# An RWKV layer and eight balanced experts on one core: where the split halves of gathered rows are kept, and where two groups of sums stand on the vector engine

## The chip, the cores and the metric

The kernel runs on one core of one Trainium2 chip. The metric is the device time of one execution in microseconds (us). Before the change it is 396.36 us, the median of three runs (396.04 to 397.14). The core's engines are named as the profile names them: PE (TensorE, matrix products), PEld (its weight loads), DVE (VectorE), ACT (ScalarE), POOL (GpSimd) and SP (SyncE, which here issues DMAs). Each engine works through its own instructions in the order in which they were compiled.

## The reference

Two stages follow one another. The first is an RWKV attention with a decaying state, for 4 sequences, 8 heads, 768 steps and a head width of 48:

```
for t in range(S):
    cur = einsum('bhd,bhe->bhde', u * k[t], v[t])
    y[t] = einsum('bhd,bhde->bhe', r[t], state + cur)
    state = w * state + einsum('bhd,bhe->bhde', k[t], v[t])
```

Its output is laid out as 3072 rows (tokens) of 384 numbers. The second stage assigns each row to one of 8 experts, 384 rows to each, by going through all gate values in falling order and giving a row to an expert as long as the row is free and the expert isn't full. Each expert then computes two matrix products on its rows:

```
logits = x @ w_gate
order = argsort(-logits.flatten())        # greedy: row free, expert not full
for e in range(E):
    h[mask_e] = maximum(x[mask_e] @ w1[e], 0)     # 384 -> 1024
    out[mask_e] = h @ w2[e]                       # 1024 -> 384
```

## The kernel before, in words

**Stages.** In the first part, up to about 150 us, the attention, the gate and a first pick of 256 rows of one expert (called the star expert) are written in a fixed order. Then the function `run` goes through the experts in the order in which the search finds them full: number 0 (the 256 early rows), 1 to 7 with three blocks of 128 rows each, and 8, the last 128 rows of the star expert. From there on a scheduler in the compiler orders the instructions of each engine: what is written first goes first if the scheduler's own clock says that its inputs are there, and what is written later fills the gaps. `tc.issue_after(ins)` ties what is written inside it behind the instruction `ins` on that instruction's engine.

**The search** (`likely_steps`, line 1025 on) finds the next full expert: three rounds of counting, each a product `counts` on PE (lines 949 and 960) between small DVE operations, then `acc` (line 1076), the rows taken, and the product `st_ps` (lines 1080 and 1081), which gives each row its place. `tokens` (line 1396 on) turns places into row numbers: DVE makes `row`, `oh` and `vals`, PE multiplies them (`some_ps`, line 1413), DVE adds (`some`, then `part`, line 1422), PE multiplies once more (`list_ps`, line 1431), and DVE writes `tok`. Then POOL gathers the rows (line 1521) and SP loads the expert's `w1` and `w2` (line 1514). The generator `later` is advanced a step at a time while the expert before it computes; `walk` is the search object. Expert 7 needs no search (`remainder`, line 1363), only the list.

**Two sets of tiles.** `self.turns` holds two pools with one buffer per name: rows `xg`, turned rows `xT`, `w1` and `w2`. Expert n uses pool n % 2.

**Turning the rows.** PE needs the rows with the 384 features on the partitions. Experts 1 and 5 are turned by PE. For 2, 3, 4, 6, 7 and 8 `turned_by_transfers` (line 1544) does it for each block: ACT splits the 4-byte numbers into 2-byte halves (`apart`, line 1551, a pool of two buffers), a DMA transpose issued by SP writes the halves back over the rows `xg` (line 1553), and ACT joins them into `xT` (line 1558). `turn_begins` starts this and `turn` ends it. The splits and joins are tied by `behind` to the last recorded copy `self.copied`. For experts with `seven` as second layer the splits begin after the product P6. For experts 6 and 7 they begin when `progress` passes 1.3, some way into the fifteen products.

**First layer.** Experts 1, 2, 4, 5 and 8 use `hidden` (line 1641): 8 banks of plain products. Experts 3, 6 and 7 (`FIRST_BY_SEVEN`) use `hidden_by_seven` (line 1593), a scheme with seven half-size products instead of eight, done twice (p = 0 and 1). It needs five sums of the turned rows, S1 to S5 (`row_sums`, line 1576, tiles `first_S`), and four sums of `w1`, T1 to T4 (`weight_sums`, line 1565, tiles `first_T`). The order of its products is

```
FIRST = {"P1": (("a0", "b0"),), "P2": (("a1", "b2"), ("d0", "c0")), "P5": (("d1", "c1"), ("S1", "T1")), ...
FIRST_ORDER = ("P1", 0), ("P2", 0), ("P5", 0), ("P6", 0), ("P1", 1), ("P7", 0), ("P3", 0), ("P4", 0), ...
```

so the second half of the third product (line 1625, `hb_ps<-first_S,first_T`) is the first to read S1 and T1. P1's `h_ps` and P2's `hc_ps` and the first half of P5 read `xT` and `w1` alone. ACT and DVE combine the products (`kept_P`, lines 1609, 1613 and 1617).

**Second layer.** Experts 1 to 5 use `seven` for two blocks and a plain product (`o_ps`, line 1783) for the third. Experts 6 and 7 use `fifteen`: fifteen products (line 1756) in four groups on sums of the hidden layer (`HID_SUMS`, eleven sums H) and of `w2` (`W2_SUMS`, ten sums W), then 20 output sums (line 1765) on DVE. All these sums are made at line 1697. For the experts with `seven`, `SEVEN_EARLY` is one sum of the hidden layer at its half. POOL scatters the results (line 1777).

**What stands where in the program before.** While expert n computes, `row_sums` for expert n+1 is written directly after `turn`, so ahead of what is left of the search and of the list of rows that follow it; `weight_sums` for n+1 is written as soon as `progress` passes 1.1.

Of the kernel before, what the change touches and what calls it, by code (L numbers as in the profile page):

```python
# [736 lines left out]
class Assignment:  # L737
# [24 lines left out]
    def __init__(self, ctx, tc, ML, CAP, C):  # L762
        self.tc, self.nc, self.ML, self.CAP, self.C = tc, tc.nc, ML, CAP, C
# [48 lines left out]
        self.ps = ctx.enter_context(tc.tile_pool(name="s_ps", bufs=1, space=PSUM))  # L812
        self.between = lambda: None
# [211 lines left out]
    def likely_steps(self, fmax, acc, place, on_fmax=None):  # L1025
# [50 lines left out]
        nc.vector.scalar_tensor_tensor(out=acc, in0=em, scalar=fmax, in1=past, op0=ALU.is_equal, op1=ALU.mult)  # L1076
# [319 lines left out]
    def tokens(self, place, NC=None):  # L1396
# [24 lines left out]
        with nc.allow_low_precision(reason="whole numbers up to 2048"):  # L1421
            nc.vector.tensor_reduce(out=part, in_=some.rearrange("p i h -> p h i"), axis=AX.X, op=ALU.add)
# [31 lines left out]
def rwkv5_eagle_then_base_layer_balanced(  # L1454
# [34 lines left out]
    class Experts:  # L1489
# [8 lines left out]
        def open_rest(self, ctx, **how):  # L1498
# [3 lines left out]
            self.apart = pool("f_apart", 1, **how)  # L1502
# [41 lines left out]
        def turned_by_transfers(self, ahead):  # L1544
            n, xg, tok = ahead[:3]
            xT = self.turns[n % 2].tile([128, KD, CAP], F32, name="xT")
            nb, halves = tok.shape[1], []
            for c in range(nb):
                apart = self.apart.tile([128, 2, DX], U16, name="apart", bufs=2)
                with self.behind():  # L1550
                    nc.scalar.copy(apart, xg[:, c, :].bitcast(U16).rearrange("p (f h) -> p h f", h=2))
# [4 lines left out]
            for c, turned in enumerate(halves):  # L1556
                with self.behind():
                    nc.scalar.copy(xT[:, :, ts(c, 128)].bitcast(U16).rearrange("p k (t h) -> p k t h", h=2),  # L1558
                                   turned.rearrange("p (h k) t -> p k t h", h=2))
# [33 lines left out]
        def hidden_by_seven(self, x, w, progress):  # L1593
# [18 lines left out]
            def block(p, i, f, src):  # L1612
                nc.scalar.activation(hid[:, ds(f * KF // 2 + p * Q, Q), ts(i, H)], src, AF.Relu)  # L1613
# [27 lines left out]
        def hidden(self, w1, xT, m, half, progress, lead=False):  # L1641
            hid = self.h.tile([128, KF, CAP], F32, name="hid")
            for js in [range(2) if lead else range(1), *([j] for j in range(2 if lead else 1, KF))]:
# [6 lines left out]
                for j in js:  # L1650
                    nc.scalar.activation(hid[:, j, 0:m], h_ps[j][:, 0:m], AF.Relu)  # L1651
# [143 lines left out]
        def run(self, ahead, later, rows, pulls={}, xT=None):  # L1795
            xT, lead = xT or self.turn(ahead), True
            row_sums = weight_sums = None
            while ahead:
# [12 lines left out]
                none = lambda: None  # L1811
                begins = [1.3]
                due = [1.55, 1.75] if some == 2 else [0.75 + 1.15 * i / (some - 1) for i in range(some)]

                def half(hid):
                    nonlocal right
# [4 lines left out]
                    last = self.sums_of(left, self.SEVEN_EARLY)  # L1821
                    if late:
                        with tc.issue_after(last.ins):
                            right = self.seven_w2(w2)
# [8 lines left out]
                def turn():  # L1833
                    nonlocal xT, row_sums
                    if ahead:
                        xT = next(pieces) if by_transfers else self.turn(ahead)
                        if after:
                            row_sums = self.row_sums(xT)

                def progress(t):  # L1840
                    nonlocal weight_sums
                    if after and t > 1.1 and not weight_sums:
                        weight_sums = self.weight_sums(ahead[3])
                    if many and begins and t > begins[0]:
                        begins.pop()
                        turn_begins()
# [14 lines left out]
                if many:  # L1861
                    self.sums_of(left, self.HID_SUMS)
# [198 lines left out]
```

## Time and profile before

| what | value |
|---|---|
| median of three runs | 396.36 us (396.04 to 397.14) |
| the profiled execution | 396.48 us, of which the span from first to last instruction is 394.7 us |
| mean granted TensorE clock | 0.992 |
| busy: DVE, ACT, POOL | 280.8 us (71%), 188.4 us (48%), 140.4 us (36%) |
| splits `apart` | 16, 834 ns each |
| transposes issued by SP | 16, median 2.8 us from issue to landing |
| joins `xT<-xg` | 16, 919 ns each |

A timeline row gives the start in us from the span's start, the duration in us, engine, line, operation, what is written from what, its size, how many were merged into the row, and in square brackets how long the engine stood idle before it and for what. Starts of neighbouring rows tell the pace; durations overlap, since the engines are pipelined. In a view of windows the columns are: the stretch, its length, then for each engine its busy time and its number of instructions, the granted TensorE clock (1.00 is full), the DMA share, and GB/s.

### The profile page before, as it was taken

To read this page: it belongs to the slowest core of one execution; us is meant where nothing else is said; L and a number is where in the kernel's file an instruction comes from. 1 tells how busy PE (TensorE), PEld (TensorE's weight loads), DVE (VectorE), ACT (ScalarE), POOL (GpSimd) and SP (SyncE) were. 2 spreads that over 40 slices of the span, in tenths; PEclk is the share of its full clock that TensorE was granted. 3 is DMA by queue.
4 is the path that set the end of the run, shared out by engine and by line. 5 is a ranking of instruction groups with operands and counts; after the bars stand their busy time and mean duration, and the time that the engine had idled before them with its cause. 6 is when DMAs were issued, how large, how long until landed. Compare 5 with 4: busy or idle time off the path is not lost.

```text
span 394.7 us, 9805 instructions
## 1 busy us (share of the span) xinstructions
PE 375.8 (95%) x3729; PEld 303.6 (77%) x3729; DVE 280.8 (71%) x959; ACT 188.4 (48%) x468; POOL 140.4 (36%) x173
## 2 busy tenths in 40 slices
PE   8899999999999999999999799999999998999993
PEld 7678888888877766686577798558657778989981
DVE  6755777586885787986867759889378964994530
ACT  4997989888873312235225343421212533544320
POOL 7878887676732022033022121203203230041020
PEclk9999999999999999999999899999999999999998
DMA  9999999787792174644644461309209573382110
GB/s 120 159 183 182 196 198 206 159 175 147 145 317 81 42 253 165 213 169 101 238 160 103 153 247 41 80 2 330 89 22 334 145 253 148 60 317 84 23 62 27
DMA packets 108136, 60.51 MB, mean 153 GB/s; under 512 B 90032, under 2 KB 102320, under 8 KB 108080
## 3 DMA queue, kind: packets, MB, share of 16 engines
q1 hardware_dynamic: 104736, 50.35, 51.7%
q0 software_dynamic: 3104, 9.44, 7.0%
q8 instruction: 31, 0.51, 0.5%
q14 instruction: 25, 0.20, 0.2%
q10 hardware_dynamic: 240, 0.00, 0.0%
HBM read 47.20 MB, written 9.44 MB: 143 GB/s over the span
## 4 chain that ended last, share of the span: by engine, by line
PE 56%; issue 16%; DVE 9%; DMA 7%; ACT 5%; POOL 5%; POOLq 0%; another core or an unknown queue 0%; DVEq 0%; ACTq 0%
PE h_ps L1648 12%; PE y_ps L546 5%; PE g_ps L506 4%; PE pa_ps L1722 4%; PE h_ps L1625 3%; DMA xg<-apart 3%; PE hb_ps L1625 3%; DMA xg<-x_rows,tok 3%; PE e_h_ps L1891 3%; PE o_ps L1783 3%; ACT AT L496 2%; PE kT_ps L459 2%; PE kv_ps L525 2%; PE pb_ps L1722 2%; PE x_ps L596 2%
## 5 line engine op out<-in xcount | busy, mean ns | idle before, releaser
L1648 PE MATMUL h_ps<-xT,w 128*128 128x384 f32 (+1 forms) x264 | 73.0, 427 | 0.2 <-ACT hid L1651 0.2
L496 ACT ACTIVATE AT<-ident,dd 128x128 f32<-128x128 f32 x192 | 59.6, 392 | 1.9 <-DVE dd L449 1.8
L1648 PEld LDWEIGHTS h_ps<-xT,w 128*128 128x128 f32 x264 | 42.1, 191 | 20.1 <-issue 2.3
L1521 POOL DMA_INDIRECT xg<-x_rows,tok x22 | 23.0, 1046 | 94.1 <-DVE own_c L1446 33.9
L1777 POOL DMA_INDIRECT out_dram<-o_all,to x16 | 19.0, 1186 | 89.6 <-DVE o_all L1765 44.8
L1651 ACT ACTIVATE hid<-h_ps 128x384 f32<-128x384 f32 (+1 forms) x40 | 17.9, 448 | 55.0 <-PE h_ps L1648 51.3
L513 DVE COPY_PREDICATED AT<-mask,g_ps 64x512 f32<-64x512 uint8 (+1 forms) x48 | 32.4, 725 | 11.9 <-PE g_ps L506 9.8
L1783 PE MATMUL o_ps<-w,hid 128*128 128x384 f32 x96 | 33.2, 489 | 0.0
L506 PE MATMUL g_ps<-rT,kT 48*64 48x128 f32 (+1 forms) x768 | 26.3, 255 | 1.8 <-DVE AT L513 1.0
L437 POOL TENSOR_TENSOR kss<-krs,wk 128x384 f32<-128x384 f32 x24 | 24.4, 1017 | 8.2 <-DVE krs L341 5.0
L546 PE MATMUL y_ps<-AT,vts 128*64 128x128 f32 x384 | 25.7, 276 | 0.0
L1783 PEld LDWEIGHTS o_ps<-w,hid 128*128 128x128 f32 x96 | 17.6, 190 | 9.9 <-issue 0.6
L444 POOL TENSOR_TENSOR rk<-rk,u_bc 128x384 f32<-128x384 f32 x24 | 24.1, 1005 | 1.9
L443 POOL TENSOR_TENSOR rk<-krs 128x384 f32<-128x384 f32 x24 | 24.6, 1023 | 0.3 <-DMA krs<-in_r_dram 0.3
L506 PEld LDWEIGHTS g_ps<-rT,kT 48*64 48x64 f32 x768 | 20.7, 132 | 5.1 <-PE unread_ps L419 0.9
L546 PEld LDWEIGHTS y_ps<-AT,vts 128*64 128x64 f32 x384 | 20.6, 137 | 1.0 <-issue 0.5
L1613 ACT ACTIVATE hid<-kept_P 128x384 f32<-128x384 f32 x18 | 9.4, 523 | 19.9 <-DVE kept_P L1617 17.9
L478 DVE TENSOR_TENSOR rT<-rT_ps,WR 112x512 f32<-112x512 f32 x23 | 15.7, 684 | 4.2 <-PE rT_ps L459 4.2
L449 DVE TENSOR_REDUCE dd<-rk 128x8 f32<-128x384 f32 x24 | 13.1, 546 | 6.5 <-POOL rk L444 6.5
L565 ACT COPY x<-y_ps 128x512 f32<-128x512 f32 x24 | 14.1, 586 | 7.3 <-PE y_ps L546 6.2
L1558 ACT COPY xT<-xg 128x768 uint16<-128x768 uint16 x16 | 14.4, 919 | 3.9 <-DMA xg<-apart 3.7
L459 PE MATMUL rT_ps<-ident,krs 128*112 128x128 f32 x96 | 15.4, 281 | 0.5 <-ACT krs L345 0.3
(342 smaller groups left out, 853.9 us busy)
## 6 DMA issues: line engine op xcount, KB each, us to landing
w<-in_moe_w_dram SPq DMA_DIRECT2D x18, 1536.0 KB, 7.0
krs<-in_k_dram SPq DMA_DIRECT2D x24, 192.0 KB, 3.8
krs<-in_r_dram SPq DMA_DIRECT2D x24, 192.0 KB, 5.1
vts<-in_v_dram SPq DMA_DIRECT2D x24, 192.0 KB, 5.1
x_rows<-xr SPq DMA_DIRECT2D x24, 192.0 KB, 2.0
xg<-x_rows,tok POOLq DMA_INDIRECT x22, 5.0
xg<-apart SPq DMA_TRANSPOSE x16, 2.8
out_dram<-o_all,to POOLq DMA_INDIRECT x16, 2.9
```

What stands on the lines that cost most here:

```text
L437: self.nc.gpsimd.tensor_mul(self.kss[:, n % self.NS].rearrange("p (g h) d -> p g h d", g=2)[:, :, :, 0:D], src, self.wk.rearrange("p (g h) ...
L443: nc.gpsimd.tensor_mul(rk, self.krs[:, n % self.NK, 1, 0:H, 0:D], self.krs[:, n % self.NK, 0, 0:H, 0:D])
L444: nc.gpsimd.tensor_mul(rk, rk, self.u_bc)
L459: self.nc.tensor.transpose(ps[0:PD + self.D, a, :], self.pair(t, a), self.ident)
L496: nc.scalar.mul(AT[:, z, a, :], self.ident, dd[:, h:h + 1])
L506: nc.tensor.matmul(g_ps[ts(i, PD), z, a, i * PD:], kT[rows, a, ts(i, PD)], rT[rows, a, i * PD:], start=True, stop=True)
L513: nc.vector.copy_predicated(out=AT[keys, :, :, steps], mask=mask, data=g_ps[keys, :, :, steps])
L546: nc.tensor.matmul(yv[q * PD:(q + 1) * PD, o // 2, o % 2, :], lhsT, rhs, start=(o // 2, q) not in seen, stop=stop, skip_group_check=True)
L1625: nc.tensor.matmul(ps[:, q, :], w[b][:, ts(p * Q + q, 128)], x[a], start=fresh, stop=(a, b) == pairs[-1], skip_group_check=True)
L1648: nc.tensor.matmul(h_ps[j][:, at], w1[:, f, ts(j, 128)], xT[:, f, at], start=(f == 0), stop=(f == KD - 1))
L1722: nc.tensor.matmul(ps, left[a][:, j, :], right[b][:, j, :], start=(j == 0 and name in ("P1", "P2", "P5")), stop=(j == KF // 2 - 1), skip_g ...
L1783: nc.tensor.matmul(o_ps, hid[:, j, ts(c, 128)], w2[:, j, :], start=(j == 0), stop=(j == KF - 1))
```

## The change

1. The pool `apart` is gone. The halves are written into the tile of rows of the other set, the pool (n + 1) % 2: three blocks have three places, where there were two buffers.
2. `row_sums` is no longer written after `turn` when the rows are turned by transfers (so for experts 3, 6 and 7). It is written at the start of the expert itself, after the rest of the search and the list for the expert behind it have been written, and tied behind `walk.taking`: the search's `acc`, or, from expert 7 on, where `rest` is set, the list's `part`.
3. `weight_sums` is tied behind `summed`, the last sum of the layer's rows: the sum of `SEVEN_EARLY`, or the last of `HID_SUMS`.
4. Where the second layer is `fifteen`, the splits are written ahead of its products, and the first layer's copies now count as `self.copied`.

```diff
+        self.taking = nc.vector.scalar_tensor_tensor(out=acc, in0=em, scalar=fmax, in1=past, op0=ALU.is_equal,
+                                                     op1=ALU.mult)
...
     def remainder(self):
+        self.rest = True
...
-            nc.vector.tensor_reduce(out=part, in_=some.rearrange("p i h -> p h i"), axis=AX.X, op=ALU.add)
+            listing = nc.vector.tensor_reduce(out=part, in_=some.rearrange("p i h -> p h i"), axis=AX.X, op=ALU.add)
+        if self.rest:
+            self.taking = listing
...
-            self.apart = pool("f_apart", 1, **how)
...
-            nb, halves = tok.shape[1], []
-            for c in range(nb):
-                apart = self.apart.tile([128, 2, DX], U16, name="apart", bufs=2)
+            halves = self.turns[(n + 1) % 2].tile([128, NC, DX], F32, name="xg")
+            for c in range(tok.shape[1]):
+                rows, apart = xg[:, c, :].bitcast(U16), halves[:, c, :].bitcast(U16)
                 with self.behind():
-                    nc.scalar.copy(apart, xg[:, c, :].bitcast(U16).rearrange("p (f h) -> p h f", h=2))
-                turned = xg[:, c, :].bitcast(U16).rearrange("p (g t) -> p g t", t=128)
-                nc.sync.dma_start_transpose(out=turned, in_=apart.rearrange("p h f -> p (h f)"))
-                halves.append(turned)
+                    nc.scalar.copy(apart.rearrange("p (h f) -> p h f", h=2), rows.rearrange("p (f h) -> p h f", h=2))
+                nc.sync.dma_start_transpose(out=rows.rearrange("p (g t) -> p g t", t=128), in_=apart)
...
-                nc.scalar.activation(hid[:, ds(f * KF // 2 + p * Q, Q), ts(i, H)], src, AF.Relu)
+                self.copied = nc.scalar.activation(hid[:, ds(f * KF // 2 + p * Q, Q), ts(i, H)], src, AF.Relu)
...
-                sums = dict(row_sums or {}, **weight_sums) if weight_sums else None
+                ahead = next((a for a in later if a), None)
+                if weight_sums and not row_sums:
+                    with tc.issue_after(walk.taking.ins):
+                        row_sums = self.row_sums(xT)
+                sums = dict(row_sums, **weight_sums) if weight_sums else None
                 row_sums = weight_sums = None
-                ahead = next((a for a in later if a), None)
...
-                    last = self.sums_of(left, self.SEVEN_EARLY)
+                    summed = self.sums_of(left, self.SEVEN_EARLY)
...
-                        if after:
+                        if after and not by_transfers:
                             row_sums = self.row_sums(xT)
...
                     if after and t > 1.1 and not weight_sums:
-                        weight_sums = self.weight_sums(ahead[3])
-                    if many and begins and t > begins[0]:
-                        begins.pop()
-                        turn_begins()
+                        with tc.issue_after(summed.ins):
+                            weight_sums = self.weight_sums(ahead[3])
...
                 if many:
-                    self.sums_of(left, self.HID_SUMS)
+                    summed = self.sums_of(left, self.HID_SUMS)
+                    turn_begins()
                     self.fifteen(left, right, tok, rows, at_product)
```

More of the change, by code (lines that the diff above doesn't have):

```diff
@@ L762, in __init__ @@
     def __init__(self, ctx, tc, ML, CAP, C):
+        self.rest = False
         self.tc, self.nc, self.ML, self.CAP, self.C = tc, tc.nc, ML, CAP, C
@@ L1546, in turned_by_transfers @@
             xT = self.turns[n % 2].tile([128, KD, CAP], F32, name="xT")
-            nb, halves = tok.shape[1], []
-            for c in range(nb):
-                apart = self.apart.tile([128, 2, DX], U16, name="apart", bufs=2)
+            halves = self.turns[(n + 1) % 2].tile([128, NC, DX], F32, name="xg")
+            for c in range(tok.shape[1]):
+                rows, apart = xg[:, c, :].bitcast(U16), halves[:, c, :].bitcast(U16)
                 with self.behind():
-                    nc.scalar.copy(apart, xg[:, c, :].bitcast(U16).rearrange("p (f h) -> p h f", h=2))
-                turned = xg[:, c, :].bitcast(U16).rearrange("p (g t) -> p g t", t=128)
-                nc.sync.dma_start_transpose(out=turned, in_=apart.rearrange("p h f -> p (h f)"))
-                halves.append(turned)
+                    nc.scalar.copy(apart.rearrange("p (h f) -> p h f", h=2), rows.rearrange("p (f h) -> p h f", h=2))
+                nc.sync.dma_start_transpose(out=rows.rearrange("p (g t) -> p g t", t=128), in_=apart)
             yield xT
-            for c, turned in enumerate(halves):
+            for c in range(tok.shape[1]):
                 with self.behind():
                     nc.scalar.copy(xT[:, :, ts(c, 128)].bitcast(U16).rearrange("p k (t h) -> p k t h", h=2),
-                                   turned.rearrange("p (h k) t -> p k t h", h=2))
+                                   xg[:, c, :].bitcast(U16).rearrange("p (h k t) -> p k t h", h=2, k=KD))
             yield xT
@@ L1650, in hidden @@
                 for j in js:
-                    nc.scalar.activation(hid[:, j, 0:m], h_ps[j][:, 0:m], AF.Relu)
+                    self.copied = nc.scalar.activation(hid[:, j, 0:m], h_ps[j][:, 0:m], AF.Relu)
                     if j == KF // 2 - 1:
@@ L1810, in run @@
                 some = pulls.get(n, 2)
-                none = lambda: None
-                begins = [1.3]
+                none, summed = lambda: None, None
                 due = [1.55, 1.75] if some == 2 else [0.75 + 1.15 * i / (some - 1) for i in range(some)]
                 def half(hid):
-                    nonlocal right
+                    nonlocal right, summed
                     for name, (i, j) in self.BLOCKS.items():
@@ L1842, in progress @@
                     if after and t > 1.1 and not weight_sums:
[L1843 to L1846 removed]
+                        with tc.issue_after(summed.ins):
+                            weight_sums = self.weight_sums(ahead[3])
                     while due and t > due[0]:
```

2 lines of the change are left out of this document (removed).

## The prediction

> **What bounds the kernel now.** I read the page first, for the engine that is nearest to full, and then the table of waits of that engine over the part that the scheduler orders and the change touches (195 us to the end).
>
> ```profile
> PE 375.8 (95%) x3729; PEld 303.6 (77%) x3729; DVE 280.8 (71%) x959; ACT 188.4 (48%) x468; POOL 140.4 (36%) x173
> ```
> ```profile
> PE st_ps L1080 <- DVE acc L1076: 2.4, 1, 2.4
> PE h_ps L1625 <- DVE kept_P L1617: 1.1, 1, 1.1
> PE some_ps L1413 <- DVE vals L937: 0.9, 1, 0.9
> PE list_ps L1431 <- DVE part L1422: 0.5, 1, 0.5
> PE pa_ps L1722 <- ACT kept_P L1727: 0.4, 1, 0.4
> ```
>
> PE is busy 95% of the span. No product is added or removed, so only what makes PE wait, or run slowly, can give time. The columns of the second fence are total, count and longest wait in us. The first four, 4.9 us in all, fall in or just ahead of the first layers of experts 3, 6 and 7, where row sums and sums of w1 are used. The fifth is the longest of the rest. I call the three places A (expert 3, near 220 us), B (expert 6, near 318) and C (expert 7 and the layers ahead of it, 326 to 352).
>
> Next, PE's timeline at A (first the last product of the search's third count, then the products around the wait) and the granted clock in three stretches (the clock stands after the number for POOL).
>
> ```profile
> 215.07 0.22 PE L960 MATMUL counts<-wide,ones_h 128*128 128x128 f16 x1
> ```
> ```profile
> 217.12 0.81 PE L1625 MATMUL h_ps<-xT,w 128*128 128x192 f32 x4
> 217.77 0.81 PE L1625 MATMUL hc_ps<-xT,w 128*128 128x192 f32 x4
> 220.93 0.17 PE L1080 MATMUL st_ps<-acc,ones 128*128 128x24 bf16 x1 [2.35 <-DVE acc L1076]
> 220.96 0.17 PE L1081 MATMUL st_ps<-acc,rest_of 128*128 128x24 bf16 x1
> 220.98 1.13 PE L1625 MATMUL hc_ps<-xT,w 128*128 128x192 f32 x4
> 221.91 1.49 PE L1625 MATMUL hb_ps<-xT,w 128*128 128x192 f32 x4
> 223.19 1.49 PE L1625 MATMUL hb_ps<-first_S,first_T 128*128 128x192 f32 x4
> 224.47 1.04 PE L1625 MATMUL h_ps<-first_S,first_T 128*128 128x192 f32 x4
> 225.35 0.33 PE L1625 MATMUL h_ps<-xT,w 128*128 128x192 f32 x1
> ```
> ```profile
> 218.60:221.00 2.40, 0.07 (x3) 0.06 (x2) 2.29 (x16) 0.00 (x0) 0.81 (x1) 1.00 0.22 82
> 221.00:223.00 2.00, 2.00 (x10) 2.00 (x10) 1.80 (x15) 0.19 (x1) 0.00 (x0) 0.63 0.18 13
> 223.00:225.00 2.00, 2.00 (x8) 2.00 (x7) 2.00 (x9) 0.62 (x2) 0.00 (x0) 0.52 0.89 245
> ```
>
> PE idles 2.35 us, and then the clock falls to 0.63 and 0.52. Four products of this kind take 0.65 us at full pace (217.12 to 217.77). The four groups that start at 220.98 take 225.35 - 220.98 = 4.37 us instead of 4 x 0.65 = 2.60. So the gap costs 2.35 + 1.77 = 4.12 us, not 2.4.
>
> **The change part by part.** At A, this is what DVE and ACT did meanwhile:
>
> ```profile
> 217.67 0.63 DVE L1583 TENSOR_TENSOR first_S<-xT 128x192 f32<-128x192 f32 x2 [2.86 <-ACT xT L1558]
> ...
> 219.02 0.28 DVE L1061 TENSOR_SCALAR full_e<-counts 128x128 f32<-128x128 f32 x1
> ...
> 220.64 0.24 DVE L1076 SCALAR_TENSOR_TENSOR acc<-em,fmax,past 128x24 bf16<-128x24 f32 x1
> ```
> ```profile
> 207.82 1.56 ACT L1551 COPY apart<-xg 128x768 uint16<-128x768 uint16 x2
> ```
> ```profile
> 212.44 0.83 ACT L1551 COPY apart<-xg 128x768 uint16<-128x768 uint16 x1 [1.65 <-DMA xg<-apart]
> ```
>
> The five row sums take 219.02 - 217.67 = 1.35 us, after DVE had idled 2.86 us for the turned rows. The search's last chain stood behind them in DVE's order although its count was there at 215.07 + 0.22 = 215.29. That chain takes 220.88 - 219.02 = 1.86 us. With the row sums tied behind acc it ends near 215.29 + 1.86 = 217.15. PE reaches st_ps at 217.77 + 0.81 = 218.58 at the latest, so the wait goes: gain 4.12. What is late next is S1: PE wants it after P1, P2 and half of P5, at 217.12 + 4 x 0.65 = 219.7. S1 is half of the 0.63 row: near 217.6 if it follows acc at once and xT is there. If the turned rows are late, the row sums hold up behind them on DVE the rest of the search and the sums of P1 and P2; the third place for halves makes that less likely, since the third split need not wait until 212.44. It can start near 209.4, so the join behind it comes up to 3 us sooner, less what the transposes in flight take from each other (at worst all of it, and then joins end as now, at 217.6, which 219.7 still bears). At the other turns ACT merely has less to wait for: worth nothing, PE waits for none of them.
>
> The tile shared with the other set adds a wait on POOL: the next gather may not start before the transposes have read the halves, and scatters queue behind it.
>
> ```profile
> 230.03 0.99 POOL L1521 DMA_INDIRECT xg<-x_rows,tok x1 [10.62 <-DVE own_b L1445]
> ```
>
> This gather waits for the list at 230, and the transposes had landed before 217.67, as xT was joined by then: over 12 us to spare, cost nothing.
>
> At B, the row sums stood ahead of the list on DVE:
>
> ```profile
> 318.60 0.31 PE L1413 MATMUL some_ps<-vals,row 128*128 128x48 f16 x6 [0.88 <-DVE vals L937]
> ```
> ```profile
> 317.57 0.45 DVE L937 TENSOR_TENSOR oh<-hi,hi_of 128x288 f16<-128x288 int32 x1
> ...
> 318.10 0.45 DVE L937 TENSOR_TENSOR vals<-oh,number 128x288 f16<-128x288 f16 x1
> ```
>
> Behind them, oh and vals come up to 1.35 us sooner, more than the 0.88 that PE waits: gain 0.88. S1 then follows the list's part. At A's pace PE reads S1 some 2.6 us after it begins the layer; some_ps and two short DVE operations lie between, about 1 us. Cost 0, at most the 0.88 again.
>
> At C, first the sums of w1:
>
> ```profile
> 331.37 0.69 DVE L1572 TENSOR_TENSOR first_T<-w 128x512 f32<-128x512 f32 x1 [5.30 <-DMA w<-in_moe_w_dram]
> 331.98 0.55 DVE L1617 TENSOR_TENSOR kept_P<-kept_P,hc_ps 128x384 f32<-128x384 f32 x1
> ```
>
> The scheduler had let T1 of expert 7 ahead of expert 6's own additions, and DVE stood 5.30 us until w1 had landed. That is PE's wait of 1.1 for kept_P. Tied behind the last H sum it can't stand there: gain 1.1. (At A and B the tie is to one sum, which comes long before: nothing.) In exchange four T sums, 4 x 0.69 = 2.8 us, come into the stretch of the fifteen products, where DVE is full:
>
> ```profile
> 334.00:348.00 14.00, 14.00 (x131) 13.99 (x129) 13.83 (x30) 7.51 (x11) 0.00 (x0) 1.00 0.29 58
> ```
> ```profile
> 350.68 0.49 PE L1625 MATMUL hb_ps<-first_S,first_T 128*128 128x192 f32 x2
> 351.68 0.18 PE L1431 MATMUL list_ps<-part,alike 128*128 128x4 f16 x1 [0.51 <-DVE part L1422]
> ```
> ```profile
> 351.45 0.17 DVE L1422 TENSOR_REDUCE part<-some 128x4 f16<-128x16 f32 x1
> ```
>
> (The third number with a count, 13.83 of 14.00 us, is DVE.) The list's part ended at 351.62. The row sums no longer ahead of it take off 1.35, the earlier hidden layer 1.1, and the T sums add 0 to 2.8, by how many W sums of expert 7 (the same shape, not needed until its fifteen products) give way. Part ends between 349.2 and 352.0, and S1, 0.35 later, between 349.5 and 352.3. PE wants it at 350.68 - 1.1 = 349.6. So PE waits 0 to 2.7 there, in place of today's 0.51 for list_ps. I take 0.8, near the low end, because W sums are written later than T sums and rank behind them: cost 0.3 net.
>
> The splits ahead of the fifteen products go into ACT's wait for the first group of products:
>
> ```profile
> 338.22 0.59 ACT L1760 COPY res<-p_ps 128x512 f32<-128x512 f32 x1 [2.62 <-PE p_ps L1756]
> ```
>
> Three splits, 3 x 0.83 = 2.5 us, fit into its 2.62 us. Without that cover the copy would be late by at most 2.5 us, and PE has a second bank to go on. The three transposes that they release go to SP, where the next load waits for expert 6 to end: nothing. Rows turned sooner wait for the list anyway: gain 0.
>
> Sum: 4.12 + 0.88 + 1.1 - 0.3 = 5.8 us.
>
> ```profile
> span 394.7 us, 9805 instructions
> ```
>
> The profiled execution took 396.48 us (1.8 us outside its span), 0.1 above the median of 396.36, so it stands for it: 396.4 - 5.8 = 390.6 us. A measurement of this kernel tells about 0.3%, 1.2 us, from no change.
>
> **The rivals.**
>
> The clock isn't the gap's doing. The row sums' wait goes but the slow 4 us stay: 390.6 + 1.8 = 392.4. For it: only one such gap is in the profile, and waits of 1.1 and 0.9 us left the clock alone. Against: the clock is 1.00 up to the gap and falls right behind it. The Trainium skill, "TensorE: Matmul & The Clock Gate", section "HAM oscillation — how this bites in real kernels", asks only that no idle gap exceeds about 3.4 us, by which 2.35 us should not matter; the trace differs, with 0.63 and 0.52 behind it. I give this 0.08.
>
> The wait at A stays. If the scheduler, with another order to fill, puts the third count later on PE, st_ps or the products behind it wait again; A gives nothing: 390.6 + 4.1 = 394.7. For: its clock already misjudged that st_ps by 2.35 us. Against: the chain has 1.4 us to spare. 0.12.
>
> C gives back. No W sum gives way, PE waits 2.7 us for S1, over the 2.35 that slowed the clock: 2.7 + 1.77 instead of 0.8, so 390.6 + 3.7 = 394.3. 0.08. With A's wait staying as well: 398.4, or with half of one 396.4, no change by measure. 0.05.
>
> Slower: the row sums come last. They are now written after the search and the list, so on DVE anything of these that is ready outranks them. At A that work is one stretch:
>
> ```profile
> 220.88:225.85 4.97, 4.77 (x27) 0.66 0.61 172
> ```
>
> If all of its 4.77 us goes first, S1 ends at 217.15 + 4.77 + 0.35 = 222.3, 2.6 us after 219.7, past the 2.35 us that cost the clock: 2.6 + 1.77 = 4.4, which eats A's 4.12 and 0.25 more. At B the same rule costs up to the 0.88. At C it lets W sums ahead: 2.7 + 1.77 - 0.51 = 4.0, less the 1.1. Together 0.25 + 0 + 2.9 = 3.1 slower than now: 399.5. The point from which it decides: PE bears 219.7 - 217.15 - 0.35 = 2.2 us of other work between acc and S1; from 4.5 us on its wait passes 2.35 and the clock falls too. Against: the search's operations depend on one another, and DVE's row at B shows the scheduler filling such pauses (between oh and vals, 317.57 to 318.10, it had begun other work of lower rank). 0.11.
>
> **How the numbers follow.** The forecast, 390.6, has 0.56; alone it lies between 389.4 (C's 0.8 and the fifth wait's 0.4 go as well) and 392.0 (B keeps its wait and S1 at C half a us more). The rivals take 0.08, 0.12, 0.08, 0.05 and 0.11. The range from 389.4 to 395.0, the second rival's 394.7 with 0.3 for the spread of runs, leaves out the last two and a little below. Faster by over 1.2 us: 0.56 + 0.08 + 0.12 + 0.08 = 0.84; within it 0.04; slower 0.12.
>
> **What would show it.** Right: no wait of st_ps for acc near 217, the clock at 1.00 through 217 to 226, no wait of some_ps for vals, no DVE idle time for w at a first_T ahead of kept_P, three splits in a row on ACT, and PE's first read of S1 without a wait over 1 us. Wrong: a wait of hb_ps for first_S over 2 us with a clock below 0.7 behind it (row sums last), a W sum between part and S1 at C, or the low clock at A without a gap.

## The result, and the profile after

The changed kernel takes 389.69 us, the median of four runs (389.15 to 390.74), beside 396.23 us for the kernel before (396.04 to 397.14, four runs). The ratio is 0.9834 with a 95% interval of 0.9807 to 0.9861. The profiled execution took 389.4 us with a span of 387.7 us and a mean granted clock of 0.995. The forecast was 390.6, the range 389.4 to 395.0.

First the table of PE's waits of the changed kernel from 190 us on (total, count and longest wait in us):

```profile
PE pa_ps L1724 <- ACT kept_P L1729: 0.4, 1, 0.4
PE some_ps L1416 <- DVE vals L938: 0.4, 1, 0.4
PE list_ps L1436 <- DVE part L1425: 0.2, 1, 0.2
PE xT_ps L1540 <- DMA xg<-x_rows,tok: 0.2, 1, 0.2
PE h_ps L1650 <- ACT hid L1653: 0.2, 1, 0.2
```

The waits of 2.4 for `acc`, 1.1 for `kept_P` behind the load, and 0.9 for `vals` at expert 6 are gone. The one for `vals` that is left stands at expert 3 and is new. (Line numbers from 763 on are one to six higher than before.)

PE's timeline of the changed kernel at A and at the joints between the stages (start, duration, operation):

```profile
214.55 0.22 PE L961 MATMUL counts<-wide,ones_h 128*128 128x128 f16 x1
214.61 2.15 PE L1785 MATMUL o_ps<-w,hid 128*128 128x384 f32 x6
216.73 0.17 PE L1082 MATMUL st_ps<-acc,ones 128*128 128x24 bf16 x1
...
219.51 0.81 PE L1627 MATMUL hb_ps<-first_S,first_T 128*128 128x192 f32 x4
...
222.00 0.31 PE L1416 MATMUL some_ps<-vals,row 128*128 128x48 f16 x6 [0.38 <-DVE vals L938]
...
246.64 0.17 PE L1082 MATMUL st_ps<-acc,ones 128*128 128x24 bf16 x1
...
305.78 0.19 PE L1386 MATMUL st_ps<-sel,ones 128*128 128x48 bf16 x1
...
315.92 0.81 PE L1627 MATMUL hb_ps<-first_S,first_T 128*128 128x192 f32 x4
...
327.63 1.05 PE L1758 MATMUL p_ps<-w,hid 128*128 128x128 f32 x8
...
343.22 0.81 PE L1627 MATMUL hb_ps<-xT,w 128*128 128x192 f32 x4
344.24 0.18 PE L1436 MATMUL list_ps<-part,alike 128*128 128x4 f16 x1 [0.20 <-DVE part L1425]
344.28 0.57 PE L1627 MATMUL h_ps<-xT,w 128*128 128x192 f32 x2
344.69 0.81 PE L1627 MATMUL hb_ps<-first_S,first_T 128*128 128x192 f32 x4
...
356.30 1.05 PE L1758 MATMUL p_ps<-w,hid 128*128 128x128 f32 x8
```

The same joints in the kernel before, as far as the prediction did not show them:

```profile
250.81 0.17 PE L1080 MATMUL st_ps<-acc,ones 128*128 128x24 bf16 x1
...
310.05 0.19 PE L1383 MATMUL st_ps<-sel,ones 128*128 128x48 bf16 x1
...
317.24 0.49 PE L1625 MATMUL h_ps<-xT,w 128*128 128x192 f32 x2
...
321.23 0.81 PE L1625 MATMUL hb_ps<-first_S,first_T 128*128 128x192 f32 x4
...
330.51 1.46 PE L1625 MATMUL hb_ps<-first_S,w 128*128 128x192 f32 x8
...
334.45 1.05 PE L1756 MATMUL p_ps<-w,hid 128*128 128x128 f32 x8
...
363.36 1.05 PE L1756 MATMUL p_ps<-w,hid 128*128 128x128 f32 x8
```

The distance from one joint to the next tells where the time went without leaning on any wait's row:

| stretch | before | after | gain | forecast |
|---|---|---|---|---|
| A: third count (215.07, 214.55) to the next search's `st_ps` | 35.74 | 32.09 | 3.65 | 4.12 |
| from there to `st_ps` ahead of expert 6's list | 59.24 | 59.14 | 0.10 | 0 |
| B: from there to expert 6's first read of S1 | 11.18 | 10.14 | 1.04 | 0.88 |
| C: from there to expert 6's fifteen products | 13.22 | 11.71 | 1.51 | 1.1 |
| C: from there to expert 7's fifteen products | 28.91 | 28.67 | 0.24 | -0.3 |
| sum | 148.29 | 141.75 | 6.54 | 5.8 |

The span is 7.0 us shorter. Of what the table leaves, 0.52 us lies ahead of the third count, where of the change only the place of the halves plays a part, and the stretch behind the last joint is 0.06 longer. In all the profiles of this study the third count starts between 213.71 and 215.07 us, so half a us there says nothing.

DVE's timeline of the changed kernel, at A and at C:

```profile
216.44 0.24 DVE L1077 SCALAR_TENSOR_TENSOR acc<-em,fmax,past 128x24 bf16<-128x24 f32 x1
...
217.55 0.36 DVE L1585 TENSOR_TENSOR first_S<-xT 128x192 f32<-128x192 f32 x1 [0.55 <-ACT xT L1560]
...
326.54 0.55 DVE L1619 TENSOR_TENSOR kept_P<-kept_P,hb_ps 128x384 f32<-128x384 f32 x1 [0.68 <-PE hb_ps L1627]
327.68 3.70 DVE L1699 TENSOR_TENSOR H<-hid 128x512 f32<-128x512 f32 x6 [0.59 <-ACT hid L1615]
...
334.91 1.28 DVE L1574 TENSOR_TENSOR first_T<-w 128x512 f32<-128x512 f32 x2
...
344.01 0.17 DVE L1425 TENSOR_REDUCE part<-some 128x4 f16<-128x16 f32 x1
344.10 0.62 DVE L1585 TENSOR_TENSOR first_S<-xT 128x192 f32<-128x192 f32 x2
```

At A `acc` goes ahead of the row sums and the first row sum waits for nothing but the joined rows. At C no T sum stands ahead of expert 6's additions and H sums, and at expert 7 the list's part goes ahead of S1, which PE then reads at 344.69.

The clock of the changed kernel in the stretch behind `st_ps` at A (the 1.00 behind the number for POOL):

```profile
218.00:220.00 2.00, 2.00 (x15) 2.00 (x14) 2.00 (x15) 0.29 (x1) 0.98 (x1) 1.00 0.64 110
220.00:222.00 2.00, 1.62 (x10) 1.40 (x10) 2.00 (x5) 1.34 (x3) 0.00 (x0) 1.00 1.01 366
222.00:224.00 2.00, 2.00 (x18) 1.85 (x18) 2.00 (x12) 0.58 (x3) 0.00 (x0) 1.00 1.07 406
```

### The profile page after: what moved, and what is told of

It reads as the page before. It is cut to its first block, busy times and chain, and to the rows that moved or that the text cites. A ratio compares the mean times of both kernels' runs of the same rounds, so it can differ in the third digit from the quotient of the medians.

```text
span 387.7 us, 9819 instructions
## 1 busy us (share of the span) xinstructions
PE 371.7 (96%) x3729; PEld 299.8 (77%) x3729; DVE 280.0 (72%) x959; ACT 187.4 (48%) x468; POOL 141.2 (36%) x173
## 4 chain that ended last, share of the span: by engine, by line
PE 56%; issue 16%; DVE 9%; POOL 7%; DMA 6%; ACT 2%; SPq 1%; POOLq 1%; another core or an unknown queue 0%; DVEq 0%
PE h_ps L1650 12%; PE y_ps L546 5%; PE pa_ps L1724 5%; PE o_ps L1785 4%; PE g_ps L506 4%; PE e_h_ps L1894 3%; PE pb_ps L1724 3%; PE h_ps L1627 3%; PE hb_ps L1627 2%; DMA xg<-x_rows,tok 2%; PE kv_ps L525 2%; PE x_ps L596 2%; PE kT_ps L459 2%; PE rT_ps L459 2%; DVE H L1699 2%
## 5 line engine op out<-in xcount | busy, mean ns | idle before, releaser
L1779 POOL DMA_INDIRECT out_dram<-o_all,to x16 | 19.8, 1234 | 88.4 <-DVE o_all L1767 43.1
L1724 PE MATMUL pa_ps<-T,S 128*128 128x192 f32 x80 | 15.8, 331 | 0.0
```

The lines of the kernel that those rows point to most:

```text
L1724: nc.tensor.matmul(ps, left[a][:, j, :], right[b][:, j, :], start=(j == 0 and name in ("P1", "P2", "P5")), stop=(j == KF // 2 - 1), skip_g ...
```

## The experiments

The theory after the result: the two ties bring all of it, the row sums' tie at A and B and the tie of the sums of `w1` at C; the third place for halves and the early splits bring nothing; and a part of A's gain is the clock, which falls behind PE's gap. The rivals: the third place is needed to have the rows in time; C gives back; the clock's fall has another cause than the gap. Each group of runs stands beside the kernel before on its own chip: 394.6 us in the first group, 394.9, 395.0 and 395.0 in the others. Times of different groups are compared by ratio, or where the kernels before agree within 0.2 us.

**The four parts alone.** Each is the kernel before with one item of the change's list (the part of the diff that belongs to it), the first:

```diff
-                apart = self.apart.tile([128, 2, DX], U16, name="apart", bufs=2)
+            halves = self.turns[(n + 1) % 2].tile([128, NC, DX], F32, name="xg")
```

> Only the halves in the other set's tile (three places in place of two); everything else as before. The prediction cost this at nothing. My theory, from the trace of after, where the three splits stand in a row but the joins at expert 3 end at 217.5 as before: the transposes are served one after another, so a third place for halves gives nothing: same as before, 396.2 within 0.5, three splits in a row on ACT, transposes landing no sooner, the wait of st_ps for acc still about 2.35. Rival: the third place brings the joins forward by up to 3 us; then the row sums at expert 3 come sooner, the wait of 2.35 with its slow clock goes, and the time is near 392.

Measured: 397.19 us, ratio 1.007 (1.005 to 1.0091): 0.7% slower, which neither expected. The profile's waits of PE:

```profile
PE st_ps L1080 <- DVE acc L1076: 2.7, 1, 2.7
...
PE list_ps L1431 <- DVE part L1422: 1.2, 1, 1.2
```

Both rows are longer than before, by 0.3 and 0.7, and yet `st_ps` starts as long behind the third count as before (5.87 us, before 5.86) and `list_ps` as long behind the first of the fifteen products (17.25, before 17.23): PE has fewer product instructions ahead of them, by two and by four. By the joints of the table the stretch A is 0.17 us longer and the one up to expert 7's fifteen products 0.59. The three splits do stand in a row on ACT, as in the changed kernel, but the last join doesn't end sooner. What grew is the time that a transpose takes from issue to landing. The kernel before, then the changed kernel, shortest, median and longest of 16:

```profile
DMA to landing us min/median/max: 2.7/2.8/3.7
```
```profile
DMA to landing us min/median/max: 2.8/4.0/4.1
```

In the kernel with the halves alone the median is 3.1, in a second profile of the changed kernel 3.5. Over all the profiles of this study it is 3.1 to 4.0 in the seven with three places and 2.8 in each of the seven with two. The last joins at expert 3 on ACT, before and after:

```profile
216.72 0.92 ACT L1558 COPY xT<-xg 128x768 uint16<-128x768 uint16 x1 [0.21 <-DMA xg<-apart]
```
```profile
215.59 1.93 ACT L1560 COPY xT<-xg 128x768 uint16<-128x768 uint16 x2 [2.45 <-DMA xg<-xg]
```

They end 217.64 - 215.07 = 2.57 us behind the third count before, and 217.52 - 214.55 = 2.97 in the changed kernel. With the halves alone it is 2.57, in the second profile of the changed kernel 2.43. In all the profiles it is 2.56 to 2.74 with two places and 2.43 to 2.97 with three, so the third place makes the last join at most 0.3 us earlier and up to 0.4 later. The two longer stretches are 0.8 us of the 2.5 that this kernel loses. All six of its executions have the slow clock that is told of below, which in the kernel before comes in some; against those the loss is 2.4 (their median in this group is 394.79). The rest isn't explained by the one profile, which is also the fastest of the six (396.42), and stays open.

The second part alone:

```diff
+                if weight_sums and not row_sums:
+                    with tc.issue_after(walk.taking.ins):
+                        row_sums = self.row_sums(xT)
...
-                        if after:
+                        if after and not by_transfers:
```

> Only the row sums tied behind the search (behind the list where the search is done). My theory: it alone removes the gap at expert 3 with its slow clock (4.1 by the prediction's reckoning, 3.7 by the two traces) and the wait of some_ps for vals at expert 6 (0.9): 391.2 to 391.7, no wait of st_ps for acc, clock 1.00 there. The wait of kept_P behind the load of w at expert 7 stays, as does list_ps or a wait for S1. Rival (the row sums need the third place for halves to be in time): the gap returns as a wait of the first read of S1 at expert 3, and the time is 393 to 396.

Measured: 390.00 us, ratio 0.9884 (0.9865 to 0.9903), 4.6 us gained. From the third count to the next `st_ps` it takes 31.72, against 35.74; at A PE waits for neither `st_ps` nor S1 nor `vals`. The wait behind the load stays:

```profile
PE h_ps L1630 <- DVE kept_P L1622: 1.2, 1, 1.2
PE pa_ps L1727 <- ACT kept_P L1732: 0.4, 1, 0.4
PE list_ps L1436 <- DVE part L1425: 0.4, 1, 0.4
```

So the third place isn't needed: the last join ends 2.60 us behind the third count here, as in the kernel before, and the 0.38 of `vals` that the changed kernel's profile shows isn't there.

The third part alone:

```diff
-                        weight_sums = self.weight_sums(ahead[3])
+                        with tc.issue_after(summed.ins):
+                            weight_sums = self.weight_sums(ahead[3])
```

> Only the sums of w1 tied behind the layer's row sums. My theory: the 5.3 us that DVE stands for w ahead of expert 6's additions go, and PE's wait of 1.1 for kept_P with them: 395.1; the gap at expert 3 stays. Since the row sums stay ahead of the search and the list, the T sums that move into the stretch of the fifteen products may make list_ps or S1 at expert 7 later: up to 0.5 of it given back. Rival (C gives all of it back): 396.2 or above, with a wait at expert 7 in place of the 1.1.

Measured: 393.37 us, ratio 0.9965 (0.9949 to 0.9981), 1.3 us gained. C doesn't give back. And its profile has PE's gap at A as in the kernel before, 2.35 us, with no fall of the clock behind it:

```profile
218.00:220.00 2.00, 0.06 (x1) 0.00 (x0) 1.90 (x12) 0.00 (x0) 0.89 (x1) 1.00 0.26 97
220.00:222.00 2.00, 1.59 (x11) 1.59 (x11) 2.00 (x17) 0.00 (x0) 0.00 (x0) 1.00 0.01 2
222.00:224.00 2.00, 2.00 (x14) 1.78 (x13) 2.00 (x11) 1.49 (x4) 0.00 (x0) 1.00 0.78 175
```

From `st_ps` to the next search's `st_ps` it takes 28.20 us here and 250.81 - 220.93 = 29.88 in the kernel before: the fall costs 1.68, close to the 1.77 of the prediction, but it isn't there in every execution.

The fourth part alone:

```diff
+                    turn_begins()
                     self.fifteen(left, right, tok, rows, at_product)
```

> Only the turn of expert 7's rows (splits ahead of the fifteen products of expert 6). With two places for halves the third split still waits for a transpose to land. My theory: same as before, 396.2 within 0.5: rows turned sooner wait for the list or the search anyway. Rival: the split that waits for a transpose stands ahead of the copies of the fifteen products on ACT and makes PE wait for a bank: slower by up to 2.

Measured: 394.84 us, ratio 1.0005 (0.999 to 1.002): no difference.

**The changed kernel, without halves, and the rival of late row sums.** The first is the changed kernel itself, the second lacks the part on the halves. The third ties the row sums behind the list at expert 3 too:

```diff
-        if self.rest:
-            self.taking = listing
+        self.taking = listing
```

> The changed kernel itself once more, beside the kernels without one of its parts. Expected: 6.5 under the kernel before where the slow clock at expert 3 is paid, 5 where it isn't; no fall of the clock near 220 in any run, so the spread of the times is that of the search and the early part alone (about 1).

> The change without its part on the halves (two places for halves, as before). My theory after the single parts: the third place brings nothing, and at expert 3 it even makes the last join 0.4 later (2.97 us after the search's third count instead of 2.57 to 2.60), which is the wait of 0.38 of some_ps for vals. Without it that wait goes: 0.4 faster than the changed kernel, within what can be measured, and the row sums start 0.4 sooner. Rival: the other parts need the third place (the splits ahead of the fifteen products have one split that waits for a transpose to land, with the copies of PE's banks behind it on ACT): 0.5 to 2 slower than the changed kernel.

> The changed kernel, but at expert 3 too the row sums stand behind the list's part instead of behind the search's taking: the rival 'row sums come last' made true at one place. By the trace of the changed kernel the list's part would end near 221.9 without row sums ahead of it, S1 near 222.2, and PE wants S1 at 219.5, less 0.65 for a product block that can go ahead: a wait of 1.8 to 2.4 there and 391.5 to 392.1; if the clock falls behind it as it did behind the gap of 2.35, 1.7 more in the executions where it falls: up to 393.8. The prediction's rival says that it needs 4.5 us of other work ahead of S1 to lose everything; here it is about 4.7 us behind acc, so the rival's 4.4 of loss (394) would be the upper end. If PE reads S1 without a wait, the point from which the rival decides was wrong.

Measured: the changed kernel 388.67 us, ratio 0.9846 (0.9825 to 0.9867); without halves 388.47, ratio 0.9836 (0.9816 to 0.9857), the same by measure; rows behind the list 389.32, ratio 0.9858 (0.9837 to 0.9878). In this execution of the changed kernel PE doesn't wait for `vals` at A (31.56 from the third count to the next `st_ps`), so the 0.38 belongs to some executions only. In the third kernel DVE ends `acc` at 216.62 and begins S1 at 222.12, 5.5 us later, and PE has no wait there:

```profile
219.45 0.81 PE L1626 MATMUL h_ps<-xT,w 128*128 128x192 f32 x4
220.10 0.81 PE L1626 MATMUL hb_ps<-xT,w 128*128 128x192 f32 x4
...
220.95 1.55 PE L1626 MATMUL hc_ps<-xT,w 128*128 128x192 f32 x8
...
222.52 0.92 PE L1626 MATMUL hb_ps<-first_S,first_T 128*128 128x192 f32 x4
```

The scheduler drew products of the layer's second pass (p = 1) forward that read `xT` and `w1` alone, 0.65 + 0.65 + 1.3 us of them, so PE reads S1 only at 222.52. My expectation of 391.5 to 392.1 was wrong, and the prediction's slower rival could not have come true at A as it was worked out: it kept PE's order fixed. The 0.65 us that this kernel loses to the changed one isn't in any one wait.

**The gap and the clock.** The first try was to make PE's gap shorter by leaving three of the five row sums ahead of the search's last chain:

```diff
+                            row_sums = self.row_sums(xT, None, slice(0, 3))
```

> The kernel before with row sums behind the search, but the first three of the five at expert 3 stay ahead of the search's last chain, so that PE's gap ahead of st_ps shrinks from 2.35 to about 1.8 and nothing else changes there. In the kernel before, and with the sums of w1 alone moved, the clock fell behind the gap of 2.35 in some executions and not in others (a mean granted clock of 0.990 to 0.993 in most, 0.994 to 0.998 in the others, times 1.2 to 1.5 apart). If the gap's length decides: fewer or no executions with the fall at 1.8, the times in one cluster, 0.5 + 1.7 under the kernel before where that one pays. If any gap of over about 1.1 can bring it: two clusters 1.2 to 1.7 apart again. By a threshold near 3.4 there would be none at 1.8 and none at 2.35.

Measured: 394.05 us, ratio 0.9988 (0.997 to 1.0005). The gap did not shrink, because with another order to fill the scheduler put `st_ps` ahead of six of the eight product instructions that had stood ahead of it:

```profile
PE st_ps L1082 <- DVE acc L1077: 2.6, 1, 2.6
```

So the run doesn't tell what it was made for. It shows two groups of executions all the same, six at 393.15 to 393.54 us with a mean clock of 0.996 to 0.998, and six at 394.57 to 395.24 with 0.992 or 0.993.

Then the gap was put back into the changed kernel by itself: operations that leave the counts unchanged ahead of one search's last chain, and PE's products held behind `st_ps`, so that neither can be reordered away.

```diff
+        for _ in range(8 if self.count_of == 4 else 0):
+            nc.vector.tensor_single_scalar(out=full, in_=full, scalar=1.0, op=ALU.mult)
...
+                        with tc.issue_after(self.tie.ins) if self.tie else ExitStack():
```

> The changed kernel with TensorE's idle time at expert 3 put back by itself: four operations that leave the counts as they are (a multiplication by 1, 0.28 us each, about 0.32 from start to start) ahead of that one search's last chain on DVE, and the layer's products held behind st_ps, so that PE has to idle ahead of st_ps as in the kernel before. Four of them: a gap of about 1.3. Without a fall of the clock 388.7 + 1.3 = 390.0; where the clock falls 1.4 to 1.7 more. If the gap's length decides, no fall here (gaps of 0.9 to 1.1 left the clock alone in the kernel before): one cluster at 390.0 and clock 1.00 from 216 to 226.

> The same with eight operations: a gap of about 2.6, as in the kernel before (2.35 by the row of the wait, 2.5 by the starts). If the gap alone brings the fall, then two clusters as in the kernel before, 391.3 and 1.4 to 1.7 above it (392.9), most of the executions in the upper one. If the fall had another cause in the kernel before (what DVE or the transfers did there, say), there is one cluster at 391.3. By a threshold of 3.4: one cluster too.

> The same with twelve operations: a gap of about 3.9. If the fall becomes more frequent with the gap's length, nearly all executions have it here: 388.7 + 3.9 + 1.4 to 1.7 = 394.0 to 394.3 in one cluster. If it comes at random, whatever the length: two clusters, 392.6 and 394.2. By a threshold of 3.4 this is the first of the three with the fall.

The operations followed each other at 0.26 us, not 0.32, so the gaps are shorter than meant. `st_ps` in the three kernels:

```profile
217.70 0.17 PE L1085 MATMUL st_ps<-acc,ones 128*128 128x24 bf16 x1 [1.01 <-DVE acc L1080]
```
```profile
219.34 0.17 PE L1085 MATMUL st_ps<-acc,ones 128*128 128x24 bf16 x1 [2.06 <-DVE acc L1080]
```
```profile
219.62 0.17 PE L1085 MATMUL st_ps<-acc,ones 128*128 128x24 bf16 x1 [3.11 <-DVE acc L1080]
```

Measured: 389.80 us (389.23 to 390.32, ratio 0.9870, 0.9849 to 0.9890), 390.52 (390.03 to 392.65, ratio 0.9896, 0.9872 to 0.9920) and 393.31 (392.24 to 393.59, ratio 0.9951, 0.9931 to 0.9970). From the changed kernel's 388.67 the first two steps cost 1.1 and 1.85, about the gap; the third costs 4.6, 1.5 more than the gap. Its profile shows why (the columns are those of the windows above, the clock behind the number for POOL):

```profile
220.00:222.00 2.00, 2.00 (x11) 2.00 (x10) 2.00 (x16) 0.48 (x1) 0.00 (x0) 0.73 0.23 25
222.00:224.00 2.00, 2.00 (x8) 2.00 (x7) 2.00 (x5) 0.00 (x0) 0.00 (x0) 0.50 0.90 312
224.00:226.00 2.00, 2.00 (x18) 1.94 (x17) 0.43 (x2) 0.90 (x3) 0.00 (x0) 0.91 1.07 400
```

The price of the fall comes out the same a second time: from `st_ps` to the next search's `st_ps` it takes 31.03 us here and 29.35 in both kernels with the shorter gaps, 1.68 more. So PE's idle time brings the fall without the row sums that DVE had ahead of the search in the kernel before. This is shown at 3.11 us: the run that was to repeat the 2.35 came to 2.06 and shows no fall. Whether the transfers of that time have a part isn't shown: the DMA share during the gap is 0.21 in the kernel before, 0.07 here and 0.00 at 2.06, but it is 0.21 too in the kernel with the sums of `w1` alone, whose profile has no fall. Counting executions by their mean clock, 0.993 or less against 0.994 or more, which agrees with the fall at A in all profiles but one:

| gap by the wait's row | kernel | with low mean clock |
|---|---|---|
| none or 0.4 | changed kernel (both times) and the four others without a gap (above and below) | 1 of 30 |
| 1.01 | four operations | 0 of 5 |
| 2.06 | eight operations | 1 of 6 |
| 2.35 | before, all groups | 43 of 60 |
| 2.35 | sums of `w1` alone | 8 of 12 |
| 2.5 to 2.7 | splits alone, three sums ahead, halves alone | 21 of 30 |
| 3.11 | twelve operations | 4 of 6 |

The one at 2.06 is the profile that doesn't agree: its clock is 1.00 at A, and 0.80 and 0.77 between 12 and 20 us, where the clock can fall too; the one without a gap has no trace. Another execution at 2.06, of 392.65 us with 0.994, lies 2.1 above that kernel's median and has no trace either, so a fall there isn't excluded. So up to 2.06 no profile shows a fall behind the gap, and from 2.35 on the low clock comes in about seven of ten executions; four of six at 3.11 are too few to tell whether a longer gap makes it more frequent. In the kernel before the two groups have medians of 393.74 and 395.00, 1.26 apart. That it comes in some executions and not in all is what the prediction's one profile could not show.

**The ties alone.** Last, only the second and third part, with splits and halves as in the kernel before.

> Only the two ties: row sums behind the search or the list, sums of w1 behind the layer's row sums; the halves in two places of their own and the splits inside the fifteen products, as in the kernel before. My theory: these two bring all of it. By the two kernels that carry them alone the gains are 4.6 and 1.3, and the first one's wait of 1.2 for kept_P goes with the second: 388.5, within 0.3 of the changed kernel (388.7) and of the change without halves (388.5). Rival: splits ahead of the fifteen products are needed, because the joins otherwise come between the copies of PE's banks and row sums and the list's part at expert 7 come later: 0.3 to 1 slower, as a wait for list_ps or S1 there.

Measured: 388.58 us (387.82 to 388.79), ratio 0.9837 (0.9815 to 0.9860), the same as the changed kernel's 0.9846. The two other parts contribute nothing that can be measured. No kernel of the study is measurably faster than the changed one.

## Why the prediction was right, step by step

The direction and the mechanism held, and the sum was 0.7 us short of the joints' 6.54.

*A, 4.12.* Measured 3.65 in the profile of after, with its new wait of 0.38, and 4.18 in the second profile of the same kernel (35.74 - 31.56). Of the 4.18 the gap is 2.50 (34.06 in the kernel with the sums of `w1` alone, which had the gap and no fall, less 31.56) and the fall 1.68. `acc` ended 216.44 + 0.24 - 214.55 = 2.13 us behind the third count, and the forecast was 217.15 - 215.07 = 2.08. But PE's order was not the one that the forecast kept: the scheduler put `st_ps` ahead of all the layer's products, right behind the six `o_ps` of 214.61. At the pace of the kernel before (217.12 - 215.13 = 1.99) these are done at 216.60, `acc` ends at 216.68, and `st_ps` starts at 216.73. So of the "1.4 us to spare" nothing was left, and that PE lost only 0.1 us there is luck: the search's last chain is about as long as those six products. Taking the clock's 1.77 as part of the gap's price was right for the profiled execution and for the median, but the prediction took as certain what comes in seven executions of ten. As a mean over executions it is 0.7 x 1.26 = 0.9. The rival "the clock isn't the gap's doing" falls: without the gap the clock is 1.00 at A, and idle time of 3.11 us put back brings the fall. But its basis, that waits of 1.1 and 0.9 leave the clock alone, was sound: 1.01 us put back did so too. The Trainium skill, "TensorE: Matmul & The Clock Gate", section "HAM oscillation — how this bites in real kernels", would have only gaps above about 3.4 us matter; here falls came behind rows of 2.35 to 3.11 us, so the measurement decides against it. The same page of the Trainium skill says in the section "What's actually happening" that the window in which the activity is watched runs freely and doesn't start anew with the kernel. That would suit a fall in seven executions of ten; no run here shows the window.

*The third place, up to 3 us sooner, "at worst all of it" lost again.* This bound failed, though the sum had nothing for it. "What the transposes in flight take from each other" was to be at most all of the gain. In the profile of after it was more: a median of 4.0 us instead of 2.8 to land, and the last join at A 0.4 later. Alone the third place made a slower kernel. In the changed kernel the row sums' tie covers it, since PE wants S1 only at 219.51.

*B, 0.88.* Measured 1.04. The row of a wait counts from the modelled end of the product ahead; by starts the two products at 317.24 are done after 0.33, at 317.57, and the wait to 318.60 is 1.03. S1 came in time, as the prediction had it.

*C, 1.1 for `kept_P`.* Measured 1.51, of which the wait by starts is 333.04 - (330.51 + 1.30) = 1.23 (eight products at 0.1625 from start to start). The other 0.28 isn't in any one row.

*C, 0.3 given back.* Wrong in sign: 0.24 gained. `part` starts 344.01 - 327.63 = 16.38 us behind the first of the fifteen products, against 351.45 - 334.45 = 17.00 before. Four T sums stand behind that product in place of one (3 x 0.6 = 1.8 us more); the row sums left (1.35) and one W sum gave way (five instead of six ahead of `part`, 0.6). That leaves 0.15 of the 0.62; the rest isn't traced to single rows. S1 was ready at 344.10 + 0.35 = 344.45, 0.58 us after PE would have wanted it, at 343.22 + 0.65 = 343.87, so its lateness was within what was forecast. The step that failed is that PE would stand still for it, 0.8 us in place of 0.51: the forecast kept PE's order fixed. The scheduler put `list_ps` and two products of the layer's second pass, which read `xT` and `w1` alone, ahead of the first read of S1. So PE waits 0.20 for `list_ps` and not for S1.

*Costed at nothing.* The tie of T sums at A and B and the splits ahead of the fifteen products cost and bring nothing, as the runs with single parts show (with the sums of `w1` alone B takes 11.18 us as before; the splits alone have a ratio of 1.0005). The tile shared with the other set, with its wait for POOL's gather, costs nothing in the changed kernel, which without halves is the same by measure. Alone it comes with the 2.5 us that are open above.

## What to carry to other kernels

On an engine that works in order, write what only the next stage needs behind the chain that releases the bottleneck engine now, and tie it there if the scheduler's clock can misjudge when an input lands; two such ties were the whole gain here. Price a wait of PE from the starts of the products on both sides, not from its row, and add the slow clock behind a gap like the 2.35 us here as a cost that comes in some executions and not in others. Where a compiler orders the instructions, don't price a late input by the order of before: at expert 7, and in the run with the rows behind the list, other products filled the time. Give a further buffer to a queue of transfers only after looking whether the time to landing holds with one more in flight.

## What the runs showed of the hardware that was not expected

The fall of PE's clock behind an idle gap of 2.35 us or more comes in some executions and not in others of the same kernel: behind gaps of 1.01 and 2.06 us no profile shows it and one of 11 executions has a low mean clock, which its trace shows elsewhere; behind gaps of 2.35 to 3.11 us it is 76 of 108. One fall costs 1.68 us by two pairs of traces, at a granted clock of 0.50 for its middle. It splits the executions of an otherwise unchanged kernel into two groups 1.3 us apart (393.74 and 395.00), which is as much as a small change brings; the mean granted clock beside each time (0.994 and above, 0.993 and below) tells them apart. And DMA transposes from one queue land later with three places for halves than with two: the median from issue to landing is 3.1 to 4.0 us in the seven profiles with three and 2.8 in each of the seven with two, and the last join at expert 3 came between 0.3 us earlier and 0.4 later.
